# Soft-MoE block on one core: a shorter router tail, first loads in another order, one more turn on PE, refitted orders

## The chip, the core and the metric

The kernel runs on one core of a Trainium2 chip. The core has a matrix engine (TensorE, PE in the profile, with its weight loads as PEld), VectorE (DVE), ScalarE (ACT), GpSimd (POOL), and SyncE (SP), which here only issues DMAs. All DMAs share 16 DMA engines. The metric is the device time of one execution in microseconds, lower is better.

## What is computed

The reference chains three blocks over 1792 tokens (4 batches of 448):

```python
q_n, k_n = rmsnorm(q, g_q), rmsnorm(k, g_k)               # (4, 12, 448, 64)
attn = softmax(q_n @ k_n.T / 8) @ v                       # per batch and head
x = attn.transpose(0, 2, 1, 3).reshape(1792, 768)
logits = x @ phi                                          # (1792, 32): 8 experts x 4 slots
d = softmax(logits, over tokens);  slot_input = d.T @ x   # (32, 768)
slot_out[e] = relu(slot_input[e] @ w1[e]) @ w2[e]         # w1 768x1024, w2 1024x768
x = softmax(logits, over slots) @ slot_out
h = x @ w_in                                              # 768x2048, float64 in memory
out = (h * sigmoid(1.702 * h)) @ w_out                    # 2048x768, float64 in memory
```

## The kernel before

**Attention.** The 12 heads of 4 batches are taken as 24 pairs p = 0 to 23; two pairs make a quad (qd), whose q, k and v are loaded together (`lq`, `lk`, `v`), and six pairs make a batch b. For each pair the rows of q and k are squared, averaged, normalised and split into a high and a low fp16 part (`square`, `meansq`, `invert`, `gain`, `qn`, `kn`, `qhi`, `qlo`, `khi`, `klo`, `q2`, `k2`). They are turned (128x128 transposes) into `kt` and `qat`. `mx` multiplies the high parts on PE for the row maxima, `max` reduces them on DVE (L547) into the spare columns of a second query tile, and that tile is turned into `qbt` (`tqb`). Only then can all of the scores `sc` (L558) be made. `exp` (L562, ACT), `esum` (L565), `pv` (L577, L572), `out` (L580) follow; `sums`, `ssb`, `sumT`, `guard`, `recip` give a quad's reciprocal sums; `x` (L623, L624) turns the pair's output and multiplies it with phi, and `xmul` scales both into the tile `xl`. The score bank of `mx` is a single buffer, a pair's output tile `ot` has two.

For p = 0 and p = 23 the turn of `qbt` is eight transposes on PE (`pe_tqb`, L518) and two copies (L301, L303). For the pairs between, it is a transposing DMA that SP issues (L512).

**Router.** After a batch's six pairs, `logits` adds the heads' parts and `r_turn` to `r_add` keep a running softmax over the tokens per slot: maximum `macc`, factor `so` for the old sums, sum `zacc`, and weighted rows `pacc`, gathered by PE (`r_gather`, L882). After the last batch `w_turn` to `w_scale` combine the four lanes of each slot; `w_exp` gives the weights, `w_scale` the matrix `selw`, and `w_z` to `w_recip` the reciprocal `rz` of the denominator.

**Experts.** `siT` (L1092) holds the slot inputs. `first_half` (L1162) and `second_half` (L1203) multiply them with w1 and w2, whose tiles stream from memory in half matrices; `reload` issues the next tile's DMAs (L117, L126) where a tile was last read. `combine` makes the softmax over slots on the side, `combine_turn` turns it within expert 1. While the last tiles arrive, w_in is decoded from float64 bits (`decode64`).

**Second block.** The first 512 tokens go through a direct product (L1462) over 16 row blocks f of w_out, each decoded (`raw`, `abs`, `wd`, `whi`, `wlo`) while the block before it is multiplied. The other 1280 tokens go in five pairs of 128-row tiles by a seven-product scheme (L1615).

**What sets the order.** Nothing is scheduled by hand. Each step is an `op` with an engine, an assumed cost, a due time (plus `SHIFT` by kind), its needs and the buffer it takes. `run` plays these through and writes the instructions in the order it finds; engines then run their own queue strictly in that order. `ON` says by a letter per pair which engine (D, P, A for DVE, POOL, ACT) does a step, `HOLD` adds needs, and steps with due time `IDLE` are fillers: small products on PE that compute nothing (L393), placed where PE would wait, as long as the plan has less work in its present window than a threshold. The weights that fit before the experts start are issued early (`early`, the first `NFIRST` = 8 pieces at once, the others pair by pair).

## Time and profile before

| | us |
|---|---|
| median of 3 runs | 654.4 |
| lowest, highest | 653.06, 658.31 |
| the profiled execution | 657.85 |
| its span in the trace | 656.1 |

The profiled execution is one of its own, so times of the trace are held against 657.85, not against the median. By stage, in the trace: the loads and the first pairs until about 60 us, attention until 288 us, the router until 304 us, the experts until 397 us, the direct product until 488 us, the seven-product scheme to the end. PE's share of busy time is a poor guide here: a waiting stage and a full one are averaged, and fillers count as work. The granted clock stands at 1.00 for 2.4 GHz and 0.5 for 1.2 GHz; a mean between them says for how much of a stretch PE had which.

### The profile page before, as it was taken

The page shows a single profiled execution, that of the slowest core. Times are in us where ns is not written, and L with a number is a line of the kernel's source. Part 1 is how long each engine was busy: PE and PEld are TensorE (multiplying, and loading weights), DVE is VectorE, ACT ScalarE, POOL GpSimd, SP SyncE. Part 2 cuts the span into 40 slices and gives each one's busy share as a digit, 9 for nine tenths or more (in the row PEclk, how much of TensorE's full clock was granted, in tenths as well). Part 3 has the DMA queues.
Part 4 walks back from the last instruction along what each step waited for, and adds up shares of the span by engine and source line. Part 5 has one row for each costly group of instructions (what it writes and reads, how often), then busy time and mean ns, then how long its engine had stood idle before and what let it go on. Part 6 is the DMA issues. An engine that isn't in the chain of part 4 may idle for free.

```text
span 656.1 us, 12140 instructions
## 1 busy us (share of the span) xinstructions
PE 602.5 (92%) x4553; PEld 395.1 (60%) x4553; DVE 485.1 (74%) x896; ACT 389.3 (59%) x768; POOL 168.1 (26%) x209
## 2 busy tenths in 40 slices
PE   2799999999999999898896878999999999999997
PEld 1433444344434444354452145888889999999997
DVE  6878979999999996545453017998999987575654
ACT  3667888887877876362242007998764545353542
POOL 3677584746765573300002000000000000000000
PEclk9999999999999999897998699999999999999999
DMA  7889989799998999667999996876120000000001
GB/s 193 291 177 214 204 187 189 158 229 229 206 188 177 212 250 192 203 241 286 344 399 405 401 375 262 312 267 224 49 86 12 34 17 28 24 20 30 15 36 49
DMA packets 147947, 121.55 MB, mean 185 GB/s; under 512 B 105744, under 2 KB 126480, under 8 KB 147888
## 3 DMA queue, kind: packets, MB, share of 16 engines
q1 hardware_dynamic: 146384, 116.42, 63.9%
q10 hardware_dynamic: 1440, 4.26, 1.7%
q8 instruction: 36, 0.59, 0.4%
q14 instruction: 23, 0.19, 0.1%
q0 software_dynamic: 64, 0.10, 0.1%
HBM read 92.18 MB, written 5.51 MB: 149 GB/s over the span
## 4 chain that ended last, share of the span: by engine, by line
PE 54%; DMA 18%; DVE 9%; ACT 8%; SPq 4%; issue 3%; POOL 2%; ACTq 0%; DVEq 0%; POOLq 0%
PE y L1615 24%; PE sc L558 6%; PE pv L577 5%; DMA wr<-in_moe_w_dram 5%; DMA wr<-wr 4%; PE y L1462 4%; DMA wt<-in_moe_w_dram 4%; DMA ws<-in_moe_w_in_dram 3%; DVE wr L547 3%; PE pv L572 2%; PE mx L542 2%; PE h L1162 2%; SPq L120 2%; DMA wr<-in_k_dram 2%; DMA wr<-in_moe_w_out_dram 1%
## 5 line engine op out<-in xcount | busy, mean ns | idle before, releaser
L547 DVE TENSOR_REDUCE wr<-mx 128x2 f16<-128x896 f32 x92 | 99.9, 1086 | 14.5 <-PE mx L542 13.9
L562 ACT ACTIVATE e<-sc,esc 128x448 f32<-128x448 f32 x96 | 57.3, 633 | 11.9 <-PE sc L558 10.1
L1615 PE MATMUL y<-wo,gh 128*128 128x256 f32 x320 | 59.6, 281 | 0.0
L1541 ACT ACTIVATE gg<-f 128x512 f32<-128x512 f32 x40 | 23.9, 597 | 58.0 <-PE f L1534 56.2
L565 POOL TENSOR_TENSOR es<-es,e 128x448 f32<-128x448 f32 x37 | 44.3, 1202 | 36.5 <-ACT e L562 15.1
L558 PE MATMUL sc<-wr 128*128 128x448 f16 (+1 forms) x192 | 48.4, 365 | 3.8 <-DMA wr<-wr 2.5
L1615 PEld LDWEIGHTS y<-wo,gh 128*128 128x128 f32 x320 | 49.3, 190 | 0.0
L1615 PE MATMUL y<-wl,gh 128*128 128x256 f32 x172 | 48.4, 281 | 0.0
L1615 PE MATMUL y<-wh,gh 128*128 128x256 f32 x172 | 48.3, 281 | 0.0
L1554 DVE TENSOR_TENSOR sg<-gg 128x128 f32<-128x128 f32 x74 | 18.2, 287 | 36.9 <-ACT gg L1541 36.8
L562 ACT ACTIVATE es<-sc,esc 128x448 f32<-128x448 f32 x54 | 33.5, 636 | 19.7 <-PE sc L558 19.4
L558 PEld LDWEIGHTS <-wr 128*128 128x128 f16 (+1 forms) x256 | 19.2, 102 | 33.3 <-issue 24.9
L1615 PE MATMUL y<-wh,gl 128*128 128x256 f32 x138 | 38.7, 281 | 0.0
L425 ACT ACTIVATE wr<-wr 128x512 f32<-128x512 f32 x48 | 30.3, 638 | 13.2 <-DVE wr L1033 4.5
L1615 PE MATMUL y<-wo,gl 128*128 128x256 f32 x120 | 33.9, 282 | 0.0
L565 DVE TENSOR_TENSOR es<-es,e 128x448 f32<-128x448 f32 x35 | 25.7, 744 | 10.1 <-PE pv L577 7.7
L485 POOL TENSOR_TENSOR wr<-wr 128x512 f32<-128x512 f32 x26 | 29.7, 1160 | 11.6 <-DVE wr L478 7.4
L1615 PEld LDWEIGHTS y<-wh,gh 128*128 128x128 f32 x172 | 32.4, 188 | 0.0
L1615 PEld LDWEIGHTS y<-wl,gh 128*128 128x128 f32 x172 | 32.4, 188 | 0.0
L430 DVE TENSOR_REDUCE wr<-wr 128x16 f32<-128x1024 f32 x24 | 29.0, 1210 | 4.0 <-ACT wr L425 3.9
L1615 PE MATMUL y<-tl,gh 128*128 128x256 f32 x111 | 31.2, 281 | 0.0
L1615 PE MATMUL y<-th,gh 128*128 128x256 f32 x111 | 31.1, 281 | 0.0
(323 smaller groups left out, 1683.0 us busy)
## 6 DMA issues: line engine op xcount, KB each, us to landing
wt<-in_moe_w_dram SPq DMA_DIRECT2D x39, 512.0 KB, 7.4
wr<-in_moe_w_out_dram SPq DMA_DIRECT2D x15, 768.0 KB, 6.4
wr<-in_moe_w_dram SPq DMA_DIRECT2D x28, 384.0 KB, 7.9
wt<-in_moe_w_dram SPq DMA_DIRECT2D x16, 384.0 KB, 5.9
ws<-in_moe_w_in_dram SPq DMA_DIRECT2D x12, 512.0 KB, 4.7
wr<-in_moe_w_dram SPq DMA_DIRECT2D x10, 512.0 KB, 5.8
out_dram<-o SPq DMA_DIRECT2D x12, 384.0 KB, 2.8
wr<-in_k_dram SPq DMA_DIRECT2D x11, 384.0 KB, 5.0
```

The costliest lines, as they stand in the source:

```text
L425: nc.scalar.activation(out=sqt[p][:, 8 * i:8 * i + 8], in_=rows(p, i), func=AF.Square, scale=D ** -0.5)
L430: nc.vector.tensor_reduce(out=part(ssqt, p, 1), in_=sqt.pop(p), axis=AX.X, op=ALU.add)
L485: eng.tensor_tensor(out=n, in0=n, in1=r.to_broadcast([P, 8, D]), op=ALU.mult)
L547: nc.vector.tensor_reduce(out=lanes(of(qb_t, p), 1)[:m, h:h + n, c, 0:1], in_=MX.pop((p, g))[:m, :n, :S], axis=AX.X, op=ALU.max,)
L558: nc.tensor.matmul(out, cols(a, n, c), cols(b, n), start=first, stop=not first)
L562: nc.scalar.activation(out=E[p, h, c], in_=SC.pop((p, h, c)), func=AF.Exp, scale=esc)
L565: on(f"e{h}{c}", p)[0].tensor_tensor(out=E[p, h, 0], in0=E[p, h, 0], in1=E[p, h, c], op=ALU.add)
L577: nc.tensor.matmul(PV[p][h * D:(h + 1) * D, :], t[:, 6 * n + 3 * h + c], E[p, h, c], start=(c == 0), stop=False)
L1462: nc.tensor.matmul(Y[t, u], a[:, t * 128:(t + 1) * 128], b[:, YC[u]], start=(f == 0 and j == 0 and (u == 0 or t % 2 == 0)), stop=(f == KF ...
L1541: nc.scalar.activation(out=ggt[k, i], in_=G[k, i], func=AF.Silu, scale=1.702)
L1554: nc.vector.tensor_tensor(out=s[:, o * P:(o + 1) * P], in0=a, in1=b, op=what)
L1615: nc.tensor.matmul(out, l[:, a], r, start=fresh and x == 0, stop=last and x == 2)
```

## The change

1. **Turns.** `qbt` of pairs 1 and 22 is turned on PE too.
2. **First loads.** The early weight pieces from the sixth on (`NSTART` = 5), and v of quad 1, wait until SP has issued k of quad 2.
3. **End of attention.** x of pair 21 gets a due time ahead of everything; the last quad's `sums` wait for it on PE, and `ssb` waits for pair 23's `out` on ACT. The last batch's `logits` add pairs 18 to 21, and pairs 22 and 23 are added by one reduction and one addition (`lastlg`).
4. **Router's tail.** `macc` holds the negated maximum, so `r_more` and `r_neg` are one step; `r_old` is folded into `r_add`; `r_gather` goes by halves of the columns instead of by head; in the last batch its second half waits for `w_back`. The four steps of the denominator leave the chain and are done by `total` within expert 0.
5. **Fillers.** 90 instead of 60 in the tail, from pair 23's `out` on, in a bank of their own (`pv`), and without that threshold.
6. **ACT.** The gate function (Silu) is called once before expert 0 and once more behind `combine`.
7. **w_out.** The decoding of block 1 no longer waits for `act` of block 0.
8. **Orders.** `ON` and `SHIFT` are refitted throughout, and the steps of the seven-product scheme get shifts of their own.

```diff
...
-        gain="DDPDDDDDPDDDDDDDDPDDDDPD",
-        qn="DPPPPPPDDPPDPDDDPPPPDDPP",
-        kn="DPPDPPPDPPPDPDDDPDDDDDPD",
...
+        gain="DDPPDPPDPDDDDDDPDPDDDDPP",
+        qn="DPPPDDDDDPDDPPDDDPPPDDDP",
+        kn="DPDPDPDPPPPDPDDPPDDDPDPP",
...
-        x0="DDDAADAADDDDADDADDAADDDA",
-        x1="DAADADADDDADDAADDAADAAAA",
-        nr="DPPPPDPPPPPP",
+        x0="DDDDAADAADDDDADAAAAADADD",
+        x1="DAADADDDDDADAADDDAADDAAD",
+        nr="DPDPDPPPPPPD",
...
-    NFIRST = 8
+    NFIRST, NSTART = 8, 5
...
-        ("meansq", 2): [("qn", 0)], ("meansq", 3): [("qlo", 0)], ("lq", 1): [("v", 0)], ("v", 0): [("lq2", 0), ("lk2", 0)],
+        ("meansq", 2): [("qn", 0)], ("meansq", 3): [("qlo", 0)], ("lq", 1): [("v", 0)], ("v", 0): [("lq2", 0), ("lk2", 0)], ("v", 1): [("lk", 2)],
...
-                    if real and min(real)[0] < t0 + 0.3 or worked.get(int(t0 / WINDOW), 0) > 1.2 * LEAST_WORK:
+                    if real and min(real)[0] < t0 + 0.3 or all(kind(a[2]) != "warm_r" for a in at) and worked.get(int(t0 / WINDOW), 0) > 1.2 * LEAST_WORK:
...
+    def warm_r():
+
+        if "warm" not in PV:
+            PV["warm"] = new("pv", [128, S])
+        nc.tensor.matmul(PV["warm"][:, :256], ident.bitcast(F16)[:, :128], ident.bitcast(F16), start=True, stop=True)
...
-        m, js = (SH if n == 3 else P), PB - (b == B - 1)
+        m, js = (SH if n == 3 else P), PB - 2 * (b == B - 1)
...
+    def logits_last(n):
+
+        if n == 0:
+            R["two"] = new("L2", [P, C, NS])
+            nc.vector.tensor_reduce(
+                out=R["two"], in_=XL[B - 1][:, :, :, PB - 2:, D:].rearrange("p c h j s -> p c s h j"), axis=AX.XY, op=ALU.add
+            )
+        else:
+            nc.vector.tensor_tensor(out=lg_t[:, B - 1], in0=R["two"], in1=lg_t[:, B - 1], op=ALU.add)
...
-        if p == NP - 1:
+        if p == 1 or p >= NP - 2:
...
-            u = 2 * T * qd + 2 * T + 8 + 4 * (p % 2) + 2 * c2
+            u = 2 * T * qd + 2 * T + 8 + 4 * (p % 2) + 2 * c2 - 2500 * (p == NP - 3)
...
-                [("esum", pp, h, 2) for pp in (p - 1, p) for h in range(2)] + [("exp", pp, 0, 3) for pp in (p - 1, p)],
+                [("esum", pp, h, 2) for pp in (p - 1, p) for h in range(2)] + [("exp", pp, 0, 3) for pp in (p - 1, p)]
+                + [("x", p - 2, 1)] * (p == NP - 1),
...
-    def r_more(b):
-        nc.vector.tensor_tensor(out=macc[b], in0=macc[b], in1=macc[b - 1], op=ALU.max)
...
+        if b:
+            nc.vector.scalar_tensor_tensor(
+                out=macc[b], in0=macc[b], scalar=-1.0, in1=macc[b - 1], op0=ALU.mult, op1=ALU.min
+            )
...
-    def r_old(b):
-        nc.vector.tensor_scalar(out=pacc, in0=pacc, scalar1=R["so"], scalar2=None, op0=ALU.mult)
...
-            nc.vector.tensor_tensor(out=acc, in0=part, in1=acc, op=ALU.add)
+            nc.vector.scalar_tensor_tensor(out=acc, in0=acc, scalar=R["so"], in1=part, op0=ALU.mult, op1=ALU.add)
...
+                ("r_gather", b, n), "PE", 0.8, u + 2 + n, lambda b=b, n=n: r_gather(b, n),
+                r("r_eb") + (["w_back"] if b == B - 1 and n else []), ("ms", "g", b, n), [("xl", b)],
...
-        op(("early", i), "SP", 0.68, T * p, f, needs + ([("early", i - 1)] if i else []))
+        op(("early", i), "SP", 0.68, T * p, f, needs + ([("early", i - 1)] if i else []) + [("lk", 2)] * (i == NSTART))
...
+        def total():
+            nc.vector.tensor_tensor(out=zacc, in0=wgt, in1=zacc, op=ALU.mult)
+            for c in range(C):
+                nc.tensor.matmul(tail[c * NS:(c + 1) * NS, 256:257], sel32, zacc, start=True, stop=True)
+            nc.vector.tensor_scalar(out=rz, in0=tail[:, 256:257], scalar1=1e-9, scalar2=None, op0=ALU.add)
+            nc.vector.reciprocal(out=rz, in_=rz)
...
+        nc.scalar.activation(out=bp.tile([128, 1], F32, name="warm"), in_=eps, func=AF.Silu)
...
                     if e == 0 and half == 0:
+                        total()
                         combine()
+                        nc.scalar.activation(out=bp.tile([128, 1], F32, name="warm"), in_=rz, func=AF.Silu)
...
-                    [o("raw")] + ([o("abs", h=0)] if h else []) + ([("act", work[0])] if f == 1 else []),
+                    [o("raw")] + ([o("abs", h=0)] if h else []),
...
```

## Rows read from the trace of the kernel before

**Rows 1.** The page: busy time by engine, and the chain's shares by engine
```profile
PE 602.5 (92%) x4553; PEld 395.1 (60%) x4553; DVE 485.1 (74%) x896; ACT 389.3 (59%) x768; POOL 168.1 (26%) x209
...
PE 54%; DMA 18%; DVE 9%; ACT 8%; SPq 4%; issue 3%; POOL 2%; ACTq 0%; DVEq 0%; POOLq 0%
```

**Rows 2.** Stretches: length, busy PE PEld DVE ACT POOL, clock, DMA share, GB/s
```profile
22.00:30.00 8.00, 7.44 (x38) 3.60 (x37) 7.58 (x16) 3.96 (x8) 6.58 (x10) 1.00 0.98 306
...
60.00:260.00 200.00, 194.98 (x1147) 83.26 (x1146) 186.32 (x264) 154.65 (x339) 122.80 (x132) 1.00 0.97 201
...
260.00:288.00 28.00, 25.35 (x144) 11.62 (x142) 12.71 (x17) 14.09 (x35) 6.21 (x5) 0.94 0.65 195
...
301.00:307.00 6.00, 5.36 (x52) 3.90 (x56) 2.68 (x9) 0.79 (x2) 0.57 (x2) 0.65 0.41 108
...
307.00:395.00 88.00, 72.07 (x914) 34.30 (x910) 27.86 (x72) 21.49 (x43) 3.50 (x17) 0.89 1.02 384
...
402.00:456.00 54.00, 50.44 (x318) 42.74 (x319) 49.88 (x69) 49.65 (x78) 0.00 (x0) 1.00 0.82 290
...
488.00:652.00 164.00, 163.95 (x1387) 163.74 (x1387) 117.98 (x307) 77.77 (x137) 0.00 (x0) 1.00 0.07 28
```

**Rows 3.** Timeline, pair 22: start, length, engine, line, operation [idle <-releaser]
```profile
259.60 1.09 DVE L547 TENSOR_REDUCE wr<-mx 64x2 f16<-64x896 f32 x1 [1.00 <-PE mx L542]
...
265.99 1.23 SPq L512 DMA_TRANSPOSE wr<-wr  x1
...
271.03 1.11 PE L558 MATMUL sc<-wr 128*128 128x448 f16 x5 [2.48 <-DMA wr<-wr]
```

**Rows 4.** The stretch of 272 to 276 us, columns as in rows 2
```profile
272.00:276.00 4.00, 4.00 (x15) 1.41 (x14) 2.14 (x4) 1.20 (x4) 0.00 (x0) 0.57 0.63 227
```

**Rows 5.** Timeline, pair 23: its turn on PE, and ACT's copy
```profile
276.01 0.61 PE L518 MATMUL ms<-ident,wr 128*128 128x128 f16 x8
...
276.94 0.60 ACT L301 ACTIVATE qbt<-ms 128x512 f16<-128x512 f16 x1
```

**Rows 6.** Waits of SP's queue in 255 to 310 us: total, times, longest
```profile
SPq L117 <- PE pv L572: 7.2, 1, 7.2
```

**Rows 7.** Timeline of the start, pairs 1 and 2
```profile
29.10 0.63 ACT L425 ACTIVATE wr<-wr 128x512 f32<-128x512 f32 x1 [0.70 <-DMA wr<-in_q_dram]
...
40.15 1.09 DVE L547 TENSOR_REDUCE wr<-mx 64x2 f16<-64x896 f32 x1
...
45.96 0.35 PE L558 MATMUL sc<-wr 128*128 128x448 f16 x1
...
54.63 0.35 PE L558 MATMUL sc<-wr,kt 128*128 128x448 f16 x1 [0.35 <-DMA wr<-wr]
```

**Rows 8.** Timeline of the router's tail and the first reload
```profile
292.35 0.56 DVE L640 TENSOR_TENSOR xl<-mx,rs 128x384 f32<-128x384 f32 x1
...
292.94 2.51 DVE L650 TENSOR_REDUCE lg<-xl 128x32 f32<-128x320 f32 x4
...
296.24 0.30 PE L841 MATMUL ms<-ident,lg 128*128 128x128 f32 x1 [1.37 <-DVE lg L658]
...
298.64 1.50 PE L882 MATMUL ms<-xl,eb 128*32 128x384 f32 x16 [0.46 <-DVE eb L877]
...
302.26 2.12 PE L1092 MATMUL h<-selw,pacc 128*128 128x32 f32 x12
...
305.45 4.59 SPq L117 DMA_DIRECT2D wt<-in_moe_w_dram  x6
```

**Rows 9.** Timeline of the first w_out blocks on PE
```profile
409.38 1.66 PE L1462 MATMUL y<-wo,gh 128*128 128x512 f32 x8 [1.25 <-ACT wo L1275]
...
429.07 1.66 PE L1462 MATMUL y<-wo,gh 128*128 128x512 f32 x8 [0.30 <-ACT wo L1275]
```

**Rows 10.** Timeline of ACT in the first expert
```profile
308.03 1.28 ACT L1107 ACT_TABLE_LOAD   x1 [1.31 <-PE h L1162]
```

**Rows 11.** Groups by line and form: busy us, mean ns of one
```profile
L485 DVE TENSOR_TENSOR wr<-wr 128x512 f32<-128x512 f32 x22 | 18.5, 857 | 0.0
```

More of the change, by code (lines that the diff above doesn't have):

```diff
@@ L89, in soft_moe_block_kernel @@
     zacc = const.tile([128, 1], F32, name="zacc")
+    wgt = const.tile([128, 1], F32, name="wgt")
     wpool_ctx = tc.tile_pool(name="wpool", bufs=NW, reuse_waits="tile")
@@ L274, in soft_moe_block_kernel @@
-        early=-1419, esum=885.5, ev=761, exp=630.4, f=612.5, fhi=789.9, flo=310.3, gain=3345.6, guard=2335.6,
-        invert=-973.2, k2=740.7, keep=795.9, khi=-1227.2, klo=-1190.9, kn=3318.5, lastlg=2716.8, ld=816.6,
-        lh=932.1, lk=21, lk2=-590.7, ll=272.6, logits=-1444.9, lq=-163.4, lq2=-1275.1, lu=336.8, lw=781.7,
-        lx=929.7, max=-652.9, meansq=-556.9, mx=-1056, out=-329.1, p=330.5, pa=731.7, pc=774.4, pe_tka=-579.6,
-        pe_tkb=1463.7, pe_tqa=1489.8, pe_tqb=-1455.5, pt=223.3, pv=-480.7, q2=1791.9, qhi=3283.5, qlo=407.3,
@@ L284, in soft_moe_block_kernel @@
-        w_exp=-1075.3, w_guard=-797.8, w_max=-549.4, w_neg=-691.3, w_recip=-21.2, w_scale=-1322.8,
-        w_sel=-307.7, w_sum=427.2, w_turn=221.7, w_z=-843.1, wd=1018.8, whi=649.9, wlo=871.7, x=1860.8,
-        xmul=3212, y=615.4, yo=948,
+        abs=2557.8, act=2556.5, arrive=-279.2, bh=871.3, bl=-19, br=334.5, bs=-176.3, cT=-779.2, close=-540.6,
+        e0=-4624.4, e1=289.6, e2=1.1, e3=1446.8, early=453.8, esum=1360.6, ev=54.4, exp=2185, f=12.6, fhi=41.9,
+        flo=-1938.9, gain=3565.3, guard=-469.8, invert=-0.8, k2=11.2, keep=-1833.3, khi=-469.1, klo=-4432.1,
@@ L665, in soft_moe_block_kernel @@
             ("ms", "warm", i), [("ms", "warm", i)],
-        )
-    for i in range(60):
-        g = ("sc", "warm_r", i)
-        op(
-            ("warm_r", i), "PE", 0.11, IDLE, lambda: warm("sc"), [("warm_r", i - 1) if i else ("exp", NP - 1, 0, 3)], g, [g],
         )
@@ L794, in soft_moe_block_kernel @@
             if p == NP - 2:
-                last.append(("x", p, 0) if c2 else ("max", NP - 1, 3))
+                last += [("x", p, 0)] if c2 else [("max", NP - 1, 3), ("sums", qd)]
             if p == NP - 1:
-                last.append(("exp", p, 0, 3))
+                last += [("exp", p, 0, 3), ("sumT", qd)]
             op(
@@ L812, in soft_moe_block_kernel @@
                 op(
-                    ("logits", b, n), "DVE", 0.76, u + 0.1 * n, lambda b=b, n=n: logits(b, n),
-                    [("xmul", PB * b + i, n // 2) for i in range(PB - last)],
+                    ("logits", b, n), "DVE", 0.5 if last else 0.76, u + 0.1 * n, lambda b=b, n=n: logits(b, n),
+                    [("xmul", PB * b + i, n // 2) for i in range(PB - 2 * last)],
                 )
-            for h, n in [(h, n) for h in range(2) for n in range(2)] if last else ():
+            for i in range(2 * last):
                 op(
-                    ("lastlg", h, n), "DVE", 0.25 if n else 0.2, u + 1, lambda h=h, n=n: logits_last(h, n),
-                    [("logits", b, i) for i in range(C)] + [("xmul", p, i) for i in range(2)] + [("lastlg", 0, n)] * h,
+                    ("lastlg", i), "DVE", 0.3 if i else 0.7, u + 1, lambda i=i: logits_last(i),
+                    [("lastlg", 0)] + [("logits", b, n) for n in range(C)] if i else [("xmul", q, n) for q in (p - 1, p) for n in range(2)],
                 )
@@ L879, in r_gather @@
     def r_gather(b, n):
-        ps = MS["g", b, n] = new("ms", [128, 6, D])
+        ps = MS["g", b, n] = new("ms", [128, 3, 2, D])
         for c in range(C):
@@ L898, in w_turn @@
     def w_turn():
-        MS["w"] = new("ms", [1, 128])
+        MS["w"] = new("sc", [1, 128])
         nc.tensor.transpose(MS["w"], macc[B - 1], ident)
@@ L921, in w_exp @@
     def w_exp():
-        nc.scalar.activation(out=rtile("wgt", [128, 1]), in_=macc[B - 1], func=AF.Exp, bias=R["nmg"], scale=1.0)
-    def w_z():
-        nc.vector.tensor_tensor(out=rtile("zs", [128, 1]), in0=R["wgt"], in1=zacc, op=ALU.mult)
-    def w_sum():
-        MS["w"] = new("ms", [128, 1])
-        for c in range(C):
-            nc.tensor.matmul(MS["w"][c * NS:(c + 1) * NS], sel32, R["zs"], start=True, stop=True)
-    def w_guard():
-        nc.vector.tensor_scalar(out=rtile("zt", [128, 1]), in0=MS.pop("w"), scalar1=1e-9, scalar2=None, op0=ALU.add)
-    def w_recip():
-        nc.vector.reciprocal(out=rz, in_=R["zt"])
+        nc.scalar.activation(out=wgt, in_=macc[B - 1], func=AF.Exp, bias=R["nmg"], scale=-1.0)
     def w_scale():
-        nc.vector.tensor_scalar(out=selw, in0=sel32, scalar1=R["wgt"], scalar2=None, op0=ALU.mult)
+        nc.vector.tensor_scalar(out=selw, in0=sel32, scalar1=wgt, scalar2=None, op0=ALU.mult)
     op("w_sel", "DVE", 0.2, 100, w_sel, [("exp", 4, 0, 0)])
@@ L956, in soft_moe_block_kernel @@
         w_last = nm
-    op("w_scale", "DVE", 0.1, T * NP + 26, w_scale, ["w_exp"])
     for b in range(B):
```

103 lines of the change are left out of this document (48 added, 55 removed).

## Prediction, made before the changed kernel was run

> **What bounds the kernel now.** I read the page's busy shares and chain first [rows 1]: PE is busy 92% of the span, but only 54% of the chain is PE and 18% is DMA, so PE's share is an average over stages that have different limits. The table of stretches [rows 2] parts them. In 60 to 260 us (attention in its steady run) PE has 194.98 of 200 us and DVE 186.32: PE is the limit and DVE is close behind it. In 260 to 288 us, the end of attention, PE has 25.35 of 28 at a mean granted clock of 0.94, while DVE and ACT have half. In 301 to 307 us, where the router ends, the loads run at 108 GB/s, and in 307 to 395 us (the experts) at 384 GB/s with PE at a mean clock of 0.89: the weight stream is the limit there. In 402 to 456 us DVE (49.88 of 54), ACT (49.65) and PE (50.44) are all nearly full. In 488 to 652 us PE has 163.95 of 164 us. So an edit pays where it moves PE's work in attention, or where it keeps the weight stream running; from 402 us on a saving on one engine alone is doubtful, and the last 164 us can't shrink by an order.
>
> **Pair 22 is turned on PE (the largest term).** The last maximum of pair 22 ends at 259.60 + 1.09 = 260.7 us. Its transposing DMA is issued only at 265.99, behind weight loads on SP's queue, and the second half of that pair's scores starts on PE at 271.03, after 2.48 us in which PE waited for this DMA [rows 3]. After the wait PE runs at the lower of its levels: in 272 to 276 us the mean granted clock is 0.57 [rows 4], so 4.00 x 0.43 = 1.7 us of PE's time go to the 1.2 GHz level. On PE the same turn is eight transposes, 0.61 us, and two copies, ACT's 0.60 us among them [rows 5], right after 260.7. ACT and DVE are half idle in this stretch, so the copies are covered. Saved: 2.48 + 1.7 - 0.6 = 3.6 us. What comes late next is pair 23, whose own turn is already on PE and whose maxima wait on PE only.
>
> **x of pair 21 is drawn ahead.** Its two steps now come before pair 23's last pv instead of behind it. Each is two transposes and two small products in fp32, and the row nearest to it is the eight-transpose turn, 0.61 us [rows 5]; I take 1.2 us for the two (bounds 0 and 1.2). PE's total doesn't change, but SP's first expert load waits for that pv (7.2 us of waiting on L572) [rows 6]: the loads are released 1.2 us later than PE's gain would have it.
>
> **The start.** Pair 1's last maximum ends at 40.15 + 1.09 = 41.2, its transposing DMA lies between, and its first score starts at 45.96 [rows 7]. With 0.61 + 0.60 us for the turn and a few tenths of handing over, it would start near 42.8: 3.1 us earlier. But pair 2's scores wait for their own transposing DMA until 54.63 [rows 7], so this alone gives pair 2 nothing. The other half of the edit bears on that: three early weight loads (128x1024, 128x768 and 128x768 floats, 1.31 MB) and v of quad 1 (0.46 MB) now go behind q and k of quad 2. At the 306 GB/s of 22 to 30 us [rows 2] that is 5.8 us of loading taken from in front of them. ACT waited 0.70 us for that q at 29.10 [rows 7], and squares done earlier leave ACT room for pair 2's rounding, on which its transposes, maxima and scores hang. On SP's queue the moved loads now stand before pair 2's transposes; what of the 5.8 us is still running then comes off, and I put that bound at a loss of 1 us. I take 2.3 us, nearer to 3.1 than to the loss because the two halves help one another; bounds -1 and 3.1.
>
> **The router's tail.** The four partial sums of logits, 2.51 us on DVE, stood between the last reciprocal and the turn; now they need only pairs 18 to 21 and run while DVE would idle. From the first x step behind the reciprocal to the turn it took 296.24 - 292.35 = 3.9 us. Now, with both x steps of pair 23 moved from ACT to DVE, three x steps stand there (3 x 0.56), one reduction over two pairs, nearest to one of the four (2.51 / 4 = 0.63 us), one addition (below 0.63; I take 0.3) and the handing over (0.1): 2.7 us. Of the 1.2 us I give back 0.4, since the sums start later behind pair 21's x: 0.8 us. The maximum and its negation become one small DVE step instead of two (I take 0.2 us), the old sum is scaled inside the addition (it ran beside the gathers before, so nothing), and the weight chain's return on PE goes between the two gathers instead of behind both, which ran 1.50 us [rows 8]: half of that and one handing over, 1.0 us. The four steps of the denominator go into the first expert. The slot inputs took 2.12 us at L1092 in a stretch whose clock is 0.65 on average [rows 2, 8]; if the new fillers, which may now fill any gap, hold 2.4 GHz, they take half, and the first weight step after them too: 1.06 + 0.57 us. Sum 3.6 us, without the clock 2.0 us.
>
> **What the loads make of it.** The stream's release moves by 3.6 + 2.3 - 1.2 = 4.7 us. The first reload (305.45) [rows 8] moves by 3.6 + 2.3 + 3.6 = 9.5 us, so 4.8 us more than the stream, and the hole in 301 to 307 us closes. It is worth 6 x (384 - 108) / 384 = 4.3 us [rows 2]. Without the fillers' clock the reload gains 3.2 us on the stream and 1.1 us of the hole stays. More than the hole can't be had: a tail shorter by another us would only let PE wait for weights.
>
> **w_out.** Block 1 is decoded before block 2. PE waits 1.25 us for block 1's rounding at 409.38, which is the most this can give. But at 429.07 PE waits again for ACT [rows 9], and DVE and ACT are full in this stretch [rows 2], so an earlier start comes back to that later wait. I take 0.3 us (bounds 0 and 1.25).
>
> **The refitted orders.** Counted by the letters (without the small steps of nr), DVE loses one step over all pairs, POOL gains five and ACT loses four. PE's work is unchanged, so I take nothing, between losing what the slower rival says and winning the 5.0 us that PE idles in 60 to 260 us [rows 2].
>
> **Sum.** 4.7 + 4.3 + 0.3 = 9.3 us. The profiled execution took 657.85 us (a span of 656.1 and 1.75 around it), so it becomes 648.55. That execution is 3.45 us above the median of the runs shown; on the median, 654.4 - 9.3 = 645.1 us.
>
> **A rule against the change.** ACT loads a table for the gate function at 308.03, 1.31 us after its exponential ended, and takes 1.28 us: 2.59 us in all [rows 10]. The change calls that function once more before this exponential. The Trainium skill, page "ScalarE: Activation LUTs", section "What ACT_TABLE_LOAD costs", says that every switch to a different set costs about 1.28 us plus a drain of 1.38 us, 2.66 us together, which this trace bears out with 2.59; by it, where the two functions share no set, the change adds two switches.
>
> **Rivals.**
> 1. The loads don't restart earlier as summed: the stream is held by PE at each tile's release, not by the hole alone, or the start's 2.3 us are lost to DVE, which is at 93% in the long run. Then 4 us remain of the sum: 654.4 - 4 = 650 us. For it: the start of pair 2 hangs on a DMA. Against: 384 GB/s right after the hole.
> 2. Everything adds: the start gives 3.1, the block 1.25, and part of PE's 5.0 idle us in 60 to 260 goes as well: 9.3 + 0.8 + 0.95 + 2.5 = 13.55 us, 641 us.
> 3. The switches reach the path. ACT would switch twice before the exponential and, as now, once behind it. The first two find ACT idle; the last holds the coefficient copies for which PE waits in expert 1; if that delays the release of expert tiles by one switch, 9.3 - 2.6 = 6.7 us remain: 647.7 us. Against it: ACT had to switch there before too.
> 4. Slower: the refitted order puts one DVE step ahead of each pair's maxima. The score bank for the maxima is a single buffer, so PE's next maximum product and the pair's turn queue behind it. One step of 128x512 takes 0.857 us on DVE on average [rows 11]; over 22 pairs that is 18.9 us: 654.4 - 9.3 + 18.9 = 664 us. It decides from 9.3 / 22 = 0.42 us per pair on. For it: DVE at 93% leaves little room in 60 to 260 us. Against: the number of its steps is unchanged.
>
> **How the numbers follow.** Forecast 0.48 (642 to 649 us), rival 1 0.18, rival 2 0.15, rival 3 0.05, rival 4 0.14. The range from 639 to 655 us leaves out rival 4 and the far end of rival 2. About 1%, 6.5 us, is what a measurement of this kernel can tell from no change. Below 647.9 lie most of the forecast, rival 2 and half of rival 3: 0.62. Above 660.9 lies most of rival 4: 0.12. The rest, 0.26, is within 1%.
>
> **What would show it.** No PE wait for a transposing DMA near the end of attention and no granted 0.5 behind it; pair 1's scores near 40.5 to 43 us; loads above 350 GB/s without a hole between the router and the experts; slot inputs in 1.1 us; the stage from 488 us on as long as before (164 us). Wrong would be: a hole of the old size, PE idle in 60 to 260 us well above 5 us (rival 4), or a start of pair 2 still at 54 us (rival 1).

## The result: 1.3% slower

The changed kernel takes 662.9 us (660.2 to 664.8) against 654.3 us (653.1 to 658.3) of the kernel before, run beside it: 1.0128 of before, interval 1.0093 to 1.0164. Forecast were 645.1 us and a range of 639 to 655. Below, every ratio is to runs of the kernel before on the same chip, with its 95% interval, and a saving in us that stands beside a ratio is that share of 654.3 us.

### The profile page after: what moved, and what is told of

It reads as the page before. It is cut to its first block, busy times and chain, and to the rows that moved or that the text cites. A ratio compares the mean times of both kernels' runs of the same rounds, so it can differ in the third digit from the quotient of the medians.

```text
span 663.0 us, 12168 instructions
## 1 busy us (share of the span) xinstructions
PE 604.4 (91%) x4568; PEld 400.7 (60%) x4568; DVE 491.1 (74%) x898; ACT 386.9 (58%) x763; POOL 168.8 (25%) x204
## 4 chain that ended last, share of the span: by engine, by line
PE 58%; DMA 18%; DVE 10%; ACT 7%; issue 3%; POOL 2%; SPq 1%; ACTq 0%; POOLq 0%; DVEq 0%
PE y L1611 24%; PE sc L565 6%; PE pv L584 5%; PE y L1458 5%; DMA ws<-in_moe_w_in_dram 4%; DMA wr<-in_moe_w_dram 4%; DMA wr<-wr 3%; DMA wt<-in_moe_w_dram 3%; DVE wr L554 2%; PE mx L549 2%; DMA kt<-wr 2%; PE h L1156 2%; PE pv L579 2%; ACT e L569 2%; PE so_ps L1199 2%
## 5 line engine op out<-in xcount | busy, mean ns | idle before, releaser
L1556 ACT ACTIVATE gh<-gg 128x512 fp32r<-128x512 f32 x40 | 25.2, 630 | 59.8 <-PE y L1611 57.0
L572 POOL TENSOR_TENSOR es<-es,e 128x448 f32<-128x448 f32 x38 | 47.8, 1267 | 37.3 <-PE pv L584 17.7
L1562 DVE TENSOR_TENSOR gl<-gg,gh 128x512 fp32r<-128x512 f32 x40 | 27.6, 690 | 34.9 <-ACT gh L1556 34.8
L1537 ACT ACTIVATE gg<-f 128x512 f32<-128x512 f32 x40 | 23.8, 597 | 16.1 <-DVE gl L1562 13.2
L549 PEld LDWEIGHTS <-wr 64*128 64x128 f16 (+1 forms) x128 | 7.9, 96 | 38.2 <-issue 32.6
```

The source lines that it names most:

```text
L572: on(f"e{h}{c}", p)[0].tensor_tensor(out=E[p, h, 0], in0=E[p, h, 0], in1=E[p, h, c], op=ALU.add)
L1537: nc.scalar.activation(out=ggt[k, i], in_=G[k, i], func=AF.Silu, scale=1.702)
L1556: nc.scalar.activation(out=t, in_=src, func=AF.Copy)
L1562: nc.vector.tensor_tensor(out=t, in0=src, in1=hi.bitcast(F32), op=ALU.subtract)
```

## The profile after

The profiled execution took 664.75 us, its span is 663.0. Busy time by engine, and the chain's shares [rows 1]:

```profile
PE 604.4 (91%) x4568; PEld 400.7 (60%) x4568; DVE 491.1 (74%) x898; ACT 386.9 (58%) x763; POOL 168.8 (25%) x204
...
PE 58%; DMA 18%; DVE 10%; ACT 7%; issue 3%; POOL 2%; SPq 1%; ACTq 0%; POOLq 0%; DVEq 0%
```

They hardly differ, which is the first lesson: the shares don't show a loss of 8 us. The stretches do (columns as in [rows 2]):

```profile
60.00:260.00 200.00, 189.75 (x1093) 81.61 (x1090) 183.22 (x251) 148.36 (x325) 120.72 (x128) 1.00 0.92 195
260.00:297.20 37.20, 36.82 (x238) 16.69 (x234) 23.35 (x38) 22.95 (x55) 9.74 (x9) 1.00 0.65 197
297.20:304.00 6.80, 6.80 (x59) 4.91 (x58) 2.83 (x7) 2.10 (x6) 0.00 (x0) 1.00 0.86 313
304.00:310.20 6.20, 5.38 (x47) 3.29 (x44) 3.91 (x13) 2.40 (x6) 0.57 (x2) 1.00 1.02 412
310.20:400.40 90.20, 71.25 (x923) 36.67 (x926) 30.02 (x78) 24.61 (x49) 3.52 (x17) 0.92 1.02 388
493.00:657.00 164.00, 164.00 (x1369) 164.00 (x1368) 116.99 (x300) 74.94 (x136) 0.00 (x0) 1.00 0.08 28
```

Where [rows 2] have PE busy for 194.98 of 200 us in 60 to 260, it is now 189.75. The end of attention has no stretch of half clock any more (1.00; before 0.94, [rows 4] 0.57). Between router and experts the loads run at 412 GB/s instead of 108. And in 164 us of the last stage PE starts 1369 products where it started 1387.

PE's waits in 60 to 260 us for DVE's maxima (the tile `mx`) and for DMAs (us in total, times, longest); the kernel x3 further down, whose order is that of before up to 260 us, has the second list:

```profile
PE mx L549 <- DVE wr L554: 5.4, 9, 1.0
PE sc L565 <- DMA wr<-wr: 2.0, 2, 1.2
PE mx L549 <- DMA wr<-wr: 1.2, 1, 1.2
```

```profile
PE mx L822 <- DVE wr L827: 2.7, 3, 1.6
PE mx L822 <- DMA qat<-wr: 1.0, 1, 1.0
```

The router's tail in the changed kernel (timeline; compare [rows 8]):

```profile
304.93 0.30 PE L850 MATMUL ms<-ident,lg 128*128 128x128 f32 x1 [0.66 <-DVE lg L670]
...
307.12 1.50 PE L889 MATMUL ms<-xl,eb 128*32 128x384 f32 x16
...
308.78 1.49 PE L1078 MATMUL h<-selw,pacc 128*128 128x32 f32 x12
...
310.20 1.07 PE L1156 MATMUL h<-wt,siT 128*32 128x256 f32 x16
...
310.90 3.42 SPq L118 DMA_DIRECT2D wt<-in_moe_w_dram  x6
```

From the end of the last pv product to the first expert product it was 287.60 to 304.31, 16.7 us; now it is 297.14 to 310.20, 13.1 us. So this stretch is 3.6 us shorter, and yet the experts begin 5.9 us later: attention ends 9.5 us later, 3.6 of them already there when pair 2 starts. The experts keep that distance (the first `u` product comes at 400.42 instead of 394.30). From there to the end of the last direct product both kernels take 90.7 us, and from there to the last product the change takes 0.7 us more.

The start (the first line is the issue of the transposing DMA of pair 2's k on SP's queue; the second is the first score product of pair 2), after and before:

```profile
30.77 6.81 SPq L519 DMA_TRANSPOSE kt<-wr  x1
...
57.56 0.35 PE L565 MATMUL sc<-qat,kt 128*128 128x448 f16 x1
```

```profile
30.72 1.93 SPq L512 DMA_TRANSPOSE kt<-wr  x1
...
53.92 0.35 PE L558 MATMUL sc<-qat,kt 128*128 128x448 f16 x1
```

Time from issue to landing of that transposing DMA, the last number, after and before:

```profile
kt<-wr SPq DMA_TRANSPOSE x1, 8.9
```

```profile
kt<-wr SPq DMA_TRANSPOSE x1, 4.6
```

The 4.6 us are one trace. In the thirteen traces with before's start and an order taken from before up to there, that DMA lands 4.5 to 6.8 us after its issue, in the five with the changed one (the change, e2, e4, g1, y1) 7.8 to 8.9.

## Experiments

My theory after the two traces: turn and tail pay as forecast; the start loses 4 us, the refitted orders 6 to 8, the last stage 3 to 4. The rival: the edits themselves cost the time.

**Undoing a part and letting the planner plan again.** Four kernels, each one exchange of text:

```
e1: before, with ON and SHIFT of the change
e2: change, with ON and SHIFT of before
e3: change, without ("v", 1): [("lk", 2)] and + [("lk", 2)] * (i == NSTART)
e4: change, without bh bl br bs sact se sf sh sl ss sy in SHIFT
```

> The kernel before with the two refitted tables (ON and SHIFT) of the changed kernel and nothing else of the change. Theory: the refitted orders are what costs time. In the changed kernel PE idles 10.0 us in 60 to 260 us instead of 5.0, the pairs 3 to 21 fall about 8 us further behind, and the last stage is about 4 us longer; so this kernel takes about 654 + 6 + 4 = 664 us, with PE idle near 10 us in 60 to 260 us. Rival: the orders are neutral (as forecast: 0) and the loss comes from the edits themselves; then it takes 654 us, within 2 us, with PE idle near 5 us there.

> The changed kernel with ON and SHIFT of the kernel before; all other edits stay. Theory (orders cost about 10 us, the moved first loads about 4, turn and tail give about 7 back): 663 - 10 = 653 us, the last stage 164 us long again and PE idle near 5 us in 60 to 260 us. Rival (edits cost it, orders neutral): 663 us.

> The changed kernel without the two new waits of the first loads (early pieces from the sixth on and v of quad 1 no longer wait for k of quad 2); pair 1 is still turned on PE. Theory: the moved loads stand in front of pair 2's transposing DMAs (8.9 us from issue to the end for one of them in the changed kernel) and cost 3.6 us or more; pair 2's scores then start near 54 us instead of 57.6 and the kernel takes 659 us. Rival: pair 2 is late because of the refitted steps of its rounding or of the turn of pair 1; it still starts near 57 us and the time stays at 663 us.

> The changed kernel without the eleven new shifts of the seven-product stage (bh, bl, br, bs, sact, se, sf, sh, sl, ss, sy), so that this stage has the due times of before. In the changed kernel its products start exactly 120 ns apart (1294 of 1329), before 118.3 ns on average. Theory: the order of the stage's other steps sets this; the spacing goes back to 118.3 ns, the stage gets about 3 us shorter, 659 to 660 us. Rival: the spacing comes from something else (where the tiles lie in memory, or the chip); it stays at 120 ns and the time at 663 us.

Measured: e1 696.6 us (1.0638, 1.0594 to 1.0682), e2 694.6 (1.0613, 1.0575 to 1.0650), e3 674.7 (1.0313, 1.0277 to 1.0348), e4 663.9 (1.0157, 1.0108 to 1.0205). Neither theory said 695. Tables (ON and SHIFT) and steps were fitted to each other: before with the new tables is 42 us slower than before, the change with the old tables 32 us slower than the change, and even two waits taken away cost 12. These runs don't price a part, they price a plan that fits nothing. Two things still follow. In the change the products of the last stage start 120 ns apart, in before 118.3 ns on average. e4 differs from the change only behind attention, and has 120 ns as the change has: the new shifts of the last stage aren't the cause. And 120 ns went with the structure of the change (e2, e3, e4), 118.4 with that of before (e1).

From here on the order is frozen. The planner is replaced by a list of steps, taken from what it wrote for either kernel (x5 below, made from before's list, has before's instructions engine by engine, and those of the turn of pair 22). A list can then be cut and joined:

```diff
     def run(bufs, SLACK=SLACK):
+        by = {o[0]: o for o in ops}
+        for n in ORDERS.pop(0):
+            by.pop(n)[4]()
+        ops.clear(); names.clear()
+        return
```

**The slot.** `wgt` became a constant tile of its own (before it was one of the router's small tiles). In the two programs' tables of addresses it takes 32 bytes, and all that is allocated behind it on that side moves: the expert weights, w_in, the decoded w_out blocks 8 to 15, the sums T start at 32 modulo 64 instead of 0, attention's own tiles at 0 instead of 32.

```diff
 g1: the change
-    zacc = const.tile([128, 1], F32, name="zacc")
-    wgt = const.tile([128, 1], F32, name="wgt")
+    zw = const.tile([128, 2], F32, name="zacc")
+    zacc, wgt = zw[:, 0:1], zw[:, 1:2]
 g2: before
+    spare = const.tile([128, 1], F32, name="spare")     # and one small memset of it, as in z3, z4 and v1
```

> The changed kernel with its new constant wgt placed in the second column of zacc's tile instead of a tile of its own. A tile of one float takes a slot of 32 bytes, so in the changed kernel all that is allocated behind it on this side (expert weights, w_in, decoded w_out, the sums of the seven-product stage) starts at 32 modulo 64 where it started at 0 before; here it starts at 0 again. Nothing else differs. Theory A (the slot): the last stage's products, exactly 120 ns apart in the three runs with the changed structure and 118.3 to 118.4 ns apart in the two with the old one, go back to 118.3 ns, 1329 x 1.7 ns = 2.3 us; 660.5 us. Rival: the spacing has another cause; 120 ns and 663 us stay.

> The kernel before with one unused constant of 128x1 floats behind zacc (and a memset of it), so that everything behind it moves by 32 bytes. Theory A (the slot): the products of the last stage start 120 ns apart and the time is 654.5 + 2.3 to 3 = 657 us. Rival: 118.3 ns and 654.5 us.

g1: 659.9 us, 1.0071 (1.0037 to 1.0104). g2: 659.2 us, 1.0065 (1.0029 to 1.0101). So 32 unused bytes make the kernel before 0.65% slower, and taking them back makes the change 0.57% faster (about 0.1 to 1.1%, with the intervals of the two ratios taken as independent). 164 us of the last stage of g1, then of g2:

```profile
492.00:656.00 164.00, 164.00 (x1390) 164.00 (x1389) 119.46 (x308) 75.69 (x138) 0.00 (x0) 1.00 0.08 30
```

```profile
493.00:657.00 164.00, 164.00 (x1369) 164.00 (x1368) 116.05 (x302) 77.13 (x135) 0.00 (x0) 1.00 0.07 27
```

1390 and 1369 products at the same granted clock: 118.3 and 120.0 ns from start to start. The stage is 2.6 us longer in g2 than before (169.2 against 166.7 us from the first to the last of its products), and as much longer in the change than in g1 (167.8 against 165.2). That is 2.6 of the 4.2 us that g2's ratio stands for; its interval allows 2 to 7.

Three runs on the base of x3 (next section) say which addresses count:

```diff
 z3: a slot ahead of attention's pools
+    spare = actx.enter_context(tc.tile_pool(name="spare_p", bufs=1)).tile([128, 1], F32, name="spare")
     for tag in "rt ed xl rs0 rs L2 ca ot ssb es e v qbt kt qat".split():
 z4: a slot where w_out's blocks 8 to 15 get their place
+            cp["spare"] = poolf("spare_q", 1).tile([128, 1], F32, name="spare")
             cp["wo"] = poolf("wo", 1)
 v1: a slot at the other end (side="right"), ahead of wpoolr
```

> The kernel with old attention and new tail (x3, 651.0 us) with an unused slot of 32 bytes ahead of attention's tiles, so that these (sums of exponentials, queries, keys, outputs, xl) start at 0 modulo 64 instead of 32; expert weights and the second block stay where they are. In the kernel before with a spare slot, attention from pair 2's first score to pair 23's last took 235.5 us instead of 230.5. Theory (attention's addresses count): 3 to 5 us more, 655 us. Rival: that was one execution's DMA timing; 651 us.

> The kernel with old attention and new tail (x3, 651.0 us) with an unused slot of 32 bytes allocated at the point where w_out's decoded blocks 8 to 15 get their place, so that these, the sums of the seven-product scheme (T) and its other buffers start at 32 modulo 64 instead of 0; attention and experts stay. Theory: the products of the last stage start 120 ns apart, 1329 x 1.7 = 2.3 us, 653.3 us. Rival: 118.3 ns and 651 us, so that the spacing hangs on tiles placed before.

> The kernel with old attention and new tail (x3, 651.0 us) with an unused slot of 32 bytes at the other end of the memory, so that the activations of the second block (gh, gl, gg), the first eight decoded w_out blocks, the coefficients and attention's shared query and key tiles move from 32 to 0 modulo 64; weights and sums of the second block stay at 0. Theory 1 (each operand that starts at 32 costs): products start 118.3 ns apart or less, 648 to 651 us. Theory 2 (the two operands of a product must differ in it): 120 ns apart as in z4, 653 to 655 us.

z3: 651.0 us, 0.9930 (0.9900 to 0.9960), as x3: attention's addresses cost nothing that shows. z4: 655.5 us, 1.0002 (0.9971 to 1.0032), against 0.9937 of x3. v1: 652.1 us, 0.9972 (0.9941 to 1.0004). The last stage of z4, of v1 and of x3:

```profile
481.00:645.00 164.00, 164.00 (x1369) 164.00 (x1368) 115.97 (x302) 76.66 (x135) 0.00 (x0) 1.00 0.07 25
```

```profile
481.00:645.00 164.00, 164.00 (x1369) 164.00 (x1368) 115.88 (x302) 76.78 (x135) 0.00 (x0) 1.00 0.07 25
```

```profile
479.00:643.00 164.00, 163.35 (x1383) 163.33 (x1383) 118.26 (x307) 78.58 (x138) 0.00 (x0) 1.00 0.08 30
```

In z4 all operands of the stage start at 32 modulo 64, in v1 all at 0, and both have 120 ns and a stage of 169.2 us. (In time v1 is 0.35% above x3, which the two intervals can't tell from nothing.) In x3 some start at 0 (w_out 8 to 15, T) and some at 32 (activations, w_out 0 to 7), and it has 118.3. So a start at 32 is not what costs (theory 1 falls); 120 ns came where all had the same. Why, no run here shows, and within x3 products whose two operands start alike are hardly slower than the rest (118.5 ns for w_out 0 to 7 with the activations), so that theory 2, product by product, isn't shown either.

**Turn and tail with before's attention.** x5 is before plus the turn of pair 22; x3 is the changed code with before's start, letters and order up to pair 22's last maximum, and the change's order from there on; `wgt` lies in zacc's slot, and the second block has before's order.

```
x5: before's list, ("tqb", 22) taken out; ("pe_tqb", 22, 0), ("pe_tqb", 22, 1), ("tqb0", 22), ("tqb", 22) behind ("pv", 21, 1)
x3: before's list up to ("tqb", 22), then the change's
```

> The kernel before with its own frozen order and one edit: pair 22 is turned on PE (eight transposes and two copies behind the second pv step of pair 21) instead of by a transposing DMA. Theory: the 2.48 us wait of PE and the 1.7 us of half clock behind it go, 0.6 us of transposes come; attention ends 3.6 us earlier, and as the first expert loads wait for attention's last product, the kernel ends 3.6 us earlier: 651 us. Rival: the loads that follow don't move with it (or the wait passes to pair 23); within 1 us of 654.5.

> The order in which the planner writes the steps is frozen here: up to the last maximum of pair 22 it is that of the kernel before (its letters too, first loads and pair 1 as before), from there on that of the changed kernel: pair 22 turned on PE, x of pair 21 early, the new router tail with its fillers, total inside expert 0, the early Silu calls. The second block has the order of the kernel before, wgt lies in zacc's slot. So it is the change without its start, its refitted attention and its slot. Theory (turn and tail pay as forecast, the rest lost): -3.6 for the turn, +1.2 for x, -3.6 for the tail, so 654.5 - 6.0 = 648.5 us, no PE wait for a transposing DMA before the last scores and no hole in the loads after the router. Rival: the edits don't pay by themselves (the weight stream sets the experts' end however early they start); 653 to 655 us.

x5: 653.8 us, 0.9978 (0.9947 to 1.0010), a third of what was expected. x3: 651.0 us, 0.9937 (0.9912 to 0.9962): 4.1 us of the 6.0, and faster than before. The whole of x3's attention from pair 2 on, and its stretch between router and experts:

```profile
53.90:285.10 231.20, 225.63 (x1336) 97.19 (x1337) 204.83 (x288) 175.72 (x388) 130.44 (x139) 1.00 0.94 203
...
292.00:298.00 6.00, 5.19 (x46) 3.21 (x44) 3.82 (x13) 2.29 (x6) 0.57 (x2) 1.00 1.02 405
```

The first score of pair 2 begins at 53.9 us in before and x3, the last pv product ends at 285.06 instead of 287.60, the first expert product starts at 298.12 instead of 304.31, with the loads at 405 GB/s ahead of it. In x5, from pair 2's first score to pair 23's last takes 228.0 us instead of 230.5 (before, then x5):

```profile
53.90:284.40 230.50, 222.48 (x1301) 95.07 (x1301) 201.97 (x283) 171.98 (x377) 130.08 (x138) 0.99 0.95 205
```

```profile
56.20:284.20 228.00, 221.44 (x1309) 95.11 (x1309) 201.86 (x284) 173.01 (x378) 129.63 (x138) 1.00 0.97 204
```

The loads behind the router still have their hole in x5, and gain little: from the last pv product to the first `u` it takes 106.8 us, as in before (106.7), against 101.5 in x3. A single trace is no exact measure of these stretches: in g2, which has before's order, attention took 235.5 us, with two stretches of half clock where before has one.

**The start.**

```
y4: x3 with pair 1 turned on PE, the four steps in the place of ("tqb", 1)
y1: the change's list up to ("sc", 3, 0, 0), before's up to ("tqb", 22), then the change's; the new waits of the loads are in
```

> The kernel with old attention and new tail (x3, 651.0 us) with pair 1 turned on PE as well, the first loads as before. Theory: pair 1's scores start near 43 instead of 45.9 us, and pair 2's, which wait for their own transposing DMA (54 us), don't move: 651 us. Rival: SP has one transposing DMA less in front of those of pair 2, which then land earlier by up to 2 us: 649 us.

> The kernel with old attention and new tail (x3, 651.0 us) plus the start of the change alone: early pieces from the sixth on and v of quad 1 behind k of quad 2, pair 1 turned on PE, steps up to pair 3's first score in the changed kernel's order. Theory: in the changed kernel's traces the moved loads (early pieces and v, issued from 26 to 30 us) lie in front of pair 1's transposing DMA of k, which takes 7.8 to 8.9 us from issue to landing (30.77 to 39.68) instead of 4.7 (30.72 to 35.37); pair 2 starts at 54.9 to 57.9 us instead of 53.9 to 56.2. So 1 to 4 us later: 654 us. Rival (the forecast's term): 2.3 us gained, 648.7 us.

y4: 651.4 us, 0.9937 (0.9901 to 0.9972): nothing, as the theory said, but pair 1 didn't start earlier either (46.7 us). y1: 657.9 us, 1.0025 (0.9991 to 1.0059), 0.88% above x3. The transposing DMA that the expectation gives to pair 1 is that of pair 2's k (pairs 0 and 1 have theirs turned on PE). In y1 it waits in line again (its issue alone takes 6.31 us), pair 2 starts 3.2 us late, and the order behind it, which was not planned for that, loses 5.7 more by pair 4, in part at lower clock:

```profile
30.68 6.31 SPq L793 DMA_TRANSPOSE kt<-wr  x1
...
57.09 0.35 PE L839 MATMUL sc<-qat,kt 128*128 128x448 f16 x1
...
60.00:80.00 20.00, 16.98 (x92) 7.92 (x90) 12.95 (x19) 12.11 (x24) 9.68 (x13) 0.89 0.91 205
```

**The middle.** y2 takes before's list up to ("sc", 3, 0, 0) and the change's from there, with its letters. z1 is y2 with x3's letters; z2 is x3 with y2's letters: 46 letters differ.

> The kernel with old attention and new tail (x3, 651.0 us), but from pair 3's first score on in the refitted order and with the refitted letters of the changed kernel; the start stays old. Theory: from pair 2's first score to pair 23's last it takes 227.4 us in x3 and 235.5 to 236.0 us in the three traces with the refitted order, whatever the slot and the start; so 8 us are lost here: 659 us, with PE idle near 10 us in 60 to 260 us and nine waits for maxima instead of three. Rival (forecast: refitted orders cost nothing): 651 us.

> The kernel with the new middle (y2, 660.8 us), but with the old letters for its steps: the order in which each engine's steps are written stays the refitted one, the engine of 46 of the 300 letters goes back to that of x3. Theory (order): the refitted order puts long DVE steps straight ahead of maxima; 661 us, 8 us lost between pair 2's first score and pair 23's last as in y2 (227.4 us in x3, near 236 in y2). Rival (letters): the time goes back to x3's 651 us. A third way: order and letters fit each other, and a mix is worse than either, above 665 us.

> The kernel with old attention and new tail (x3, 651.0 us), but with the refitted letters in the middle; the order in which the steps are written is x3's. Theory (order): 651 us. Rival (letters): 660 us. Third way (they fit each other): above 660 us.

| | old letters | new letters |
|---|---|---|
| old order | x3 651.0 us, 0.9937 (0.9912 to 0.9962) | z2 657.9 us, 1.0024 (0.9996 to 1.0051) |
| new order | z1 662.4 us, 1.0104 (1.0053 to 1.0155) | y2 660.8 us, 1.0077 (1.0038 to 1.0116) |

The refitted middle costs 1.40%, 9.2 us (about 0.9 to 1.9%). With either set of letters the new order is the slower one, by 1.67% with the old and 0.53% with the new. But the letters cost too: in the old order the new ones are 0.87% slower, clear of noise, and in the new order they cost nothing that shows. The two costs don't add up, so neither theory of z2 was met, and the 9.2 us belong to order and letters together. The same 1336 products of PE, from pair 2's first score to pair 23's last pv, take 231.2 us in x3 and 242.5 in y2 (the first line; under it PE's waits in it):

```profile
54.40:296.90 242.50, 229.34 (x1336) 98.76 (x1337) 209.08 (x291) 174.29 (x386) 130.15 (x137) 1.00 0.88 193
...
PE mx L822 <- DVE wr L827: 6.3, 10, 1.4
PE sc L838 <- DMA wr<-wr: 2.6, 2, 1.3
```

13.2 us of PE idle instead of 5.6, and 3.7 us more in which it counts as busy; a product by itself takes as long (357 ns for a score product in both), so these 3.7 us are products that start further apart.

Where does it fall? The stretch from pair 2's first score to pair 17's first, then from there to pair 23's last score, in x3 and in y2:

```profile
53.90:211.10 157.20, 152.78 (x896) 64.78 (x894) 147.53 (x202) 125.53 (x274) 96.38 (x106) 1.00 0.97 199
211.10:281.30 70.20, 69.38 (x426) 31.24 (x423) 53.60 (x80) 48.85 (x112) 34.07 (x34) 1.00 0.92 221
```

```profile
54.37:223.28 168.91, 157.75 (x902) 65.63 (x901) 153.41 (x207) 124.23 (x269) 99.17 (x110) 1.00 0.90 187
223.28:293.09 69.81, 68.13 (x419) 31.96 (x417) 51.99 (x78) 48.71 (x114) 31.01 (x29) 1.00 0.87 219
```

All of it lies ahead of pair 17: 11.7 us, and nothing in the seven pairs behind. The change has the same picture (165.3 and 70.5 us, 8.1 us lost ahead of pair 17). The new letters in the old order (z2) lose 3.2 us ahead of pair 17 and 5.0 behind it.

Is it the late maxima? Ahead of most of these waits a DVE step of 0.5 to 1.7 us (`gain`, `qn`, `qlo`, `esum`) ran straight before the maximum. v2 moves eleven such steps behind it:

```diff
-... ("gain", 13), ("max", 10, 0) ...
+... ("max", 10, 0), ("gain", 13) ...
```

> The kernel with the new middle (y2, 660.8 us, 1.0077 of before) with eleven DVE steps moved from just ahead of a late maximum to just behind it (two gains, one qn, one qlo, four esum, one xmul, two recip); everything else stays in the refitted order. In y2, PE waited 7.2 us in 12 waits for maxima between 67 and 254 us. Theory (the steps ahead of the maxima cost the time): PE waits for maxima fall to 2 us or less and about 5 us come back: 655 to 656 us, 1.000 to 1.001 of before. Rival (the loss lies elsewhere in the order, and the waits pass on to the steps that were moved back): 660 us, 1.007.

```profile
54.20:297.70 243.50, 231.27 (x1336) 98.66 (x1337) 206.55 (x291) 174.67 (x385) 130.36 (x137) 0.99 0.88 193
...
PE mx L822 <- DVE wr L827: 2.8, 4, 1.0
PE mx L822 <- DMA wr<-wr: 2.2, 2, 1.9
PE sc L838 <- DMA wr<-wr: 2.1, 2, 1.3
```

v2: 661.6 us, 1.0094 (1.0061 to 1.0127). The waits for maxima fell from 6.3 to 2.8 us, but PE's idle only from 13.2 to 12.2, and the time stayed. The busy time rose by 1.9 us: behind the wait of 1.9 us for a DMA, which ends at 252.9, the granted clock is 0.50 from 253.3 to 256.7 us, which costs 1.7. So the rival holds: the waits pass on. What in the refitted middle costs the 9 us, beyond that it falls ahead of pair 17, stays open.

**The second block.** y3 is x3 with the change's list for the second block (the planner's second call), block 1 of w_out ahead of block 2.

> The kernel with old attention and new tail (x3, 651.0 us) with the changed kernel's order for the second block (refitted due times, block 1 of w_out decoded ahead of block 2). Forecast: 0.3 us gained, at most 1.25: 650.7 us. Theory from the traces: from the first product of the direct part to the first of the seven-product part it took 82.8 us and 1.7 us of products behind it in x3, and 82.4 us with the new order and the slot in place; so about 2 us gained, 649 us. Rival: the gain comes back in the last stage; 651 us.

y3: 650.8 us, 0.9920 (0.9882 to 0.9959), 0.2% below x3, which can't be told from nothing. In its trace PE's wait of 1.24 us for block 1's rounding is gone, and one of 0.82 us for the tile `ust` is new; from the first `u` to the last product it takes 257.4 us, in x3 257.2. Its time is the lowest of the study, though not to be told from x3's: the change without its start, its middle and its slot.

## Why the prediction was wrong

In shares of before, the parts add up: turn, x and tail -0.63% (x3); the refitted middle +1.40% (y2 against x3); start and second block within that order -0.06% (g1 against y2); the slot +0.57% (the change against g1). Together +1.28%. That this is the measured ratio shows nothing, since each step starts from the kernel in which the last one ended; what counts is each step's own interval, 0.25% either way for x3 and about 0.5% (3 us) for the other three. In us of 654.3: -4.1 + 9.2 - 0.4 + 3.7 = 8.4. The step of the prediction that failed is the term of nothing for the refitted orders; the slot, which it left out, and the start add to it.

- **Pair 22 on PE: right in mechanism, too large.** The 2.48 us wait and the half clock are gone, as said. Attention gained 2.5 us of the 3.6 (x5), the kernel 1.4, an interval from -0.7 to 3.5. By itself it leaves the hole in the loads open.
- **x of pair 21: two sizes that cancel.** Forecast were -3.6 + 1.2 = -2.4 us at attention's end, and x3 has -2.5. But from pair 2's first score to the last pv product x3 and x5 take the same 231.2 us: the traces give 2.5 for the turn and nothing for x.
- **The tail: right in direction, its parts missed both ways.** From the release of the loads to the first reload the forecast had 3.6 + 1.2 = 4.8 us less; it is 4.1 (17.8 to 13.7). Up to the turn 0.85 us came instead of 2.0, from the gathers to the slot inputs 1.96 instead of 1.0, and from the clock 1.07 instead of 1.63: the slot inputs take 1.49 us, not 1.1, at full clock.
- **The hole in the loads: right.** 405 to 412 GB/s where 108 stood; from the last pv product to `u` 5.2 us less in x3 and 3.4 in the change, forecast 4.3. Rival 1 thus fails for the stream. Turn, x and hole were forecast at 3.6 - 1.2 + 4.3 = 6.7 us together; by its times x3 gained 4.1 (2.5 to 5.8), so as a sum they were too large. (The two traces show 8.1, but before's profiled execution is 3.6 us above its median and x3's 1.2 below.)
- **The start: right in place, wrong in size.** The moved loads "now stand before pair 2's transposes", and I put that at a loss of 1 us at most. The transpose of pair 2's k is issued at 30.77 us, behind all of them, and lands 4.3 us later than before (39.68 against 35.37). What was to be gained ahead of q and k is small: q of quad 2 lands 1.2 us earlier (27.4 us), k at the same 30.2. Of the 3.1 us for pair 1 the change has 0.7 (45.27 against 45.96), e4 with the same attention 2, g1 and y4 nothing; no trace has it by 43. In before's order the start costs 5.8 us (y1, about 3 to 8.5); in the refitted order, which was made with it, about nothing, 3 us either way (g1 against y2, with the second block's order). So no run shows that it makes the change slower, and none shows the 2.3 us.
- **w_out: not to be told.** Forecast 0.3 us; y3 against x3 is 0.17%, 1.1 us, with about 3 us either way. The mechanism is as said: one wait goes and a later one comes.
- **The refitted orders: the step that failed.** I counted steps per engine, found them nearly equal (DVE keeps its number, POOL gains five and ACT loses five; my count was off by one), and took 0. The count says nothing on where a step stands, and refitted order and letters cost 9.2 us, in the traces all of it ahead of pair 17. Rival 4 had the sign and its mark (PE idle in 60 to 260 us well above 5: 10.3), but not the mechanism: steps ahead of the maxima are there, and moving them away gives nothing back; and it is not a loss in each pair. That its time (664 us) is near the measured 662.9 is luck: it has 18.9 us lost and 9.3 gained where the runs have 9.2 lost here, 3.7 by the slot and 4.5 gained.
- **The slot: not in the list at all.** A line that declares one float per partition (`wgt`, in none of the points and printed lines of the change) goes with 3.7 us, an interval of 3 us either way; 2.6 of them show in the last stage of the traces. The forecast said that the last 164 us can't shrink by an order, and didn't ask whether they could grow by an address.
- **The switches of ACT's tables (rival 3): not on the path.** The change has three table loads between 308 and 317 us where there was one [rows 10]:

```profile
308.73 1.28 ACT L1146 ACT_TABLE_LOAD   x1 [1.23 <-PE ms L889]
...
310.24 1.28 ACT L1095 ACT_TABLE_LOAD   x1
313.56 0.63 ACT L1095 ACTIVATE lg<-lg 128x512 f32<-128x512 f32 x1 [2.04 <-DVE lg L1094]
...
315.49 1.28 ACT L1100 ACT_TABLE_LOAD   x1 [1.29 <-DVE rc L1099]
```

DVE's reciprocal that the call behind the exponential reads, before and after:

```profile
307.68 0.25 DVE L1106 RECIPROCAL rc<-nm 128x16 f32<-128x16 f32 x1
```

```profile
315.16 0.25 DVE L1099 RECIPROCAL rc<-nm 128x16 f32<-128x16 f32 x1
```

The second load is over at 311.52, and ACT then waits 2.04 us for DVE; PE's wait for the coefficient copies is the same 2.2 us in two pieces in both kernels. Each load takes 1.28 us, as the Trainium skill gives it (page "ScalarE: Activation LUTs", section "What ACT_TABLE_LOAD costs"). The drain of 1.38 us that it adds to every switch does not show as a time of its own: ACT idles 0.02 us ahead of the second load, and the 1.31 us of before, which the prediction took for the drain, end 0.1 us behind that reciprocal (307.68 + 0.25 us), as the 1.29 us ahead of the third load do. New on PE is a wait of 1.8 us for `lg` in expert 0, in the change and in x3: `total` stands on DVE ahead of `combine`, whose exponential starts 3.4 us behind the first expert product instead of 1.8. No run shows whether that costs time; PE waits 13.5 us for weights in the experts.

## What to carry to other kernels

When a planner's tables are refitted, the count of steps says nothing: price a new order by running it alone, with the list of steps frozen, and never by exchanging the tables under other steps, which cost 32 to 42 us here. A new small tile is an edit to every address behind it; put it where nothing moves, or test the shift by itself. A sum of steps that adds up to the measured total by construction proves none of them: give each its own interval. An edit at the start is worth what the next transfer in line makes of it: list all DMAs in flight when it issues.

## What the runs showed of the hardware that was not expected

- Products of 128x256 elements start 118.3 ns apart on average (nearly all between 114 and 123) when their operands' tiles start partly at 0 and partly at 32 modulo 64, and in lockstep, 120 ns each (all but 11 at most of some 1290 spacings), when all start at the same of the two, at a granted clock of 1.00 in either case. Thirteen traces of this study have the one, seven the other, and none is between.
- The transposing DMA of pair 2's k lands 4.5 to 6.8 us after its issue in thirteen traces with the old start, and 7.8 to 8.9 us in five where v and three or four weight pieces, 1.8 to 2.2 MB, are issued ahead of it; its issue then holds SP's queue for 4.6 to 6.8 us instead of 1.9.
- With the same order up to that point, pair 2's first score came between 53.5 and 56.2 us in twelve traces with the old start, and between 54.9 and 57.9 in four with the new one (57.6 in the change, 54.9 in e4, whose attention is the same program): executions of one order differ by some 2.5 us there, so one trace can't price an edit of a microsecond at the start.
